# A first MLP product in two pieces: 256 tokens instead of 512 per matmul, in the last of six blocks

## The chip, the core and the metric

The kernel runs on one core of one Trainium2 chip. The metric is the device time of one execution in microseconds (us). Within the core five engines work side by side and meet through semaphores: TensorE (PE in the profile; its weight loads have a row of their own, PEld), VectorE (DVE), ScalarE (ACT), GpSimd (POOL) and SyncE (SP), which starts most of the transfers. Matmul results go to PSUM, which holds eight banks of 128 partitions by 512 fp32 values; everything else lies in SBUF or in DRAM.

## What is computed

The reference has two parts. The first is a Mamba-2 style state-space mixer over inputs of batch 4, 8 heads, 768 tokens, head size 32, state size 16. Cut to its core:

```python
for c in range(nc):                       # chunks of 32 tokens
    cum = np.cumsum(la, axis=-1)
    L = np.exp(cum[:, :, :, None] - cum[:, :, None, :]) * causal
    M = np.einsum('bhin,bhjn->bhij', Cc, Bc) * L
    y = np.einsum('bhij,bhjd->bhid', M, xc) + C_state_term
    state = decay_full * state + sum_of_outer_products
```

Its result, rearranged to 3072 tokens by 256 features, goes through an MLP with a hard-swish:

```python
h = x @ w_in                              # 3072 x 256 @ 256 x 2048
g = h * np.clip(h + 3.0, 0.0, 6.0) / 6.0
return g @ w_out                          # 3072 x 2048 @ 2048 x 256
```

Inputs are fp32 (the weights arrive as 64-bit floats and are decoded on the chip), and the output is fp32.

## The kernel before, in words

**Blocks.** The 768 tokens of each batch row are cut into `NC` = 6 blocks of 128, so a block holds `TB` = 512 tokens (4 batch rows by 128). Block k's mixer output `yTs[k]` is 256 features by 512 tokens, as two halves j = 0, 1 of 128 features. The 2048 hidden features are `NF` = 16 groups f of 128. While block k's MLP runs, the mixer of block k+1 is woven into it. The order on every engine is written out by hand in the loop at the end of the function (line 1030 on); nothing reorders it but the semaphores between engines.

**First MLP product.** Block 0 multiplies plain fp32 operands (`mlp_in`, line 626). Blocks 1 to 5 do it differently. `in_parts` splits each weight tile into three tiles of type F32R (`hi`, `lo`, `less`), and `split_y` does the same to the block's activations. A product of two F32R tiles is recorded as one matmul, a product of two plain fp32 tiles as two. Three such products are summed in one PSUM bank for each f: hi by hi and lo by lo (`squares`, line 696), and, after the bank has been scaled in place by `enlarge` (ACT at line 711, or DVE at line 708 for every fourth f), less by less (`cross`, line 713). Each of the three goes over j = 0, 1, so a group f takes 6 matmuls of 128x128 weights against 512 tokens, and a block 16 x 6 = 96. All of them are issued by `part_products`, line 692.

**After it.** `factor` turns the bank into the activated value: `ramp` on ACT (line 730) writes `gT`, `times_ramp` on DVE (line 735) multiplies it by the bank. Six banks are used in turn (f mod 6).

**Order in a block.** For f = 2 to 15 the loop at line 1084 issues `squares(k, f)`, `cross(k, f - 2)`, `enlarge(k, f)`, `factor(k, f - 2)`. The first two groups of a block are begun at the end of the block before it, by `lead` and `lead_on` (hi by hi, then lo by lo and the scaling): 8 matmuls for f = 0, 1.

**Second MLP product.** It is a Strassen-like scheme in which 7 products stand for 8, with sums of `gT` made on POOL (`g_sums`, line 796) and sums of `w_out` made once on DVE. Blocks 1 to 4 use `wide_units` (tiles wa, wb, wc, line 874, 256 columns per matmul). The last block uses `out_units` (tiles oa, ob, line 810, 128 columns per matmul): its activations are the stationary operand, so that its results need no turning and go straight out. It runs after the last `squares`, and the last two output transfers and one DVE addition (line 851) follow its last matmul.

**What the change touches.** `part_products` alone, called by `squares`, `cross`, `lead` and `lead_on`, for k = 5.

Of the kernel before, what the change touches and what calls it, by code (L numbers as in the profile page):

```python
# [21 lines left out]
def kernel(  # L22
# [24 lines left out]
    nc = tc.nc  # L47
    P = 128
# [3 lines left out]
    NC = S // P  # L52
    TB = NB * P
# [68 lines left out]
    FP = NF // NP  # L122
# [32 lines left out]
    def conceal_in(t, pattern):  # L155
# [24 lines left out]
        out=head, in_=head, pattern=[[-2 * N, NQ], [-N, 2]], compare_op=ALU.is_ge,  # L180
        fill=0.0, base=0, channel_multiplier=1)
    nc.gpsimd.affine_select(
        out=head, in_=head, pattern=[[2 * N, NQ], [N, 2]], compare_op=ALU.is_ge,
# [456 lines left out]
    w_parts, y_parts, hs_ = {}, {}, {}  # L640
# [47 lines left out]

    def part_products(k, f, n, m, start=False):
        w, y = w_parts[f // FP][n], y_parts[k][m]  # L690
        for j in range(NK):
            nc.tensor.matmul(  # L692
                out=hs_[k, f], lhsT=w[j][:, f % FP * P:(f % FP + 1) * P], rhs=y[:, j],
                start=(start and j == 0), stop=True, skip_group_check=True)

    def squares(k, f, low=True):

        pool, tag = ((ps, "f0"), (ps, "f1"), (ps, "f2"), (ps, "f3"), (ps_y, "y0"), (ps_y, "y1"))[f % 6]
        hs_[k, f] = pool.tile([P, TB], FP32, name="h", tag=tag)
        part_products(k, f, 0, 0, start=True)  # L700
        if low:
            part_products(k, f, 1, 1)
# [10 lines left out]
    def cross(k, f):  # L713
        part_products(k, f, 2, 2)
# [461 lines left out]
```

## Time and profile before

| what | value |
|---|---|
| three runs | 343.15, 343.79 (median), 344.34 us |
| profiled execution, its own time | 343.4 us |
| its span in the profile | 341.7 us |
| PE busy | 333.8 us, 98% of the span, 3372 matmul records and as many weight loads |
| DVE, ACT, POOL busy | 210.7, 188.3, 145.4 us |
| granted PE clock | 1.0 for the whole core |
| chain that ended last | PE 94% of the span; line 692 alone 33% |

A matmul record's duration covers the whole passage through the array, and records overlap: 480 records of line 692 last about 0.4 us each, but follow each other every 0.23 us. What a matmul costs in a dense row is therefore read from the chain that ended last (so many pieces of one line in so many us), not from the mean duration in the table of groups. The chain lists stretches as start, length, engine, tile, line and number of instructions. In the table of groups, `x160 | 51.8, 409 | 0.0` means 160 instructions, 51.8 us busy, 409 ns each, and no idle time before them. Weight loads are recorded the same way, in rows of PEld.

### The profile page before, as it was taken

How to read it: one execution, taken by the hardware profiler on the slowest of the kernel's cores; microseconds unless marked ns; L12 is line 12 of the kernel's file. 1: busy time of each engine (PE TensorE's matmuls, PEld its weight loads, DVE VectorE, ACT ScalarE, POOL GpSimd, SP SyncE). 2: the span in 40 equal slices, each digit the busy share in tenths (PEclk: the TensorE clock that was granted, in tenths of full speed). 3: DMA queues.
4: the chain of work that ended last, by engine and by line, in shares of the span. 5: the costliest groups of instructions: out<-in, count | busy, mean ns of one | idle time of the engine just before them, and what ended most of it. 6: DMA issues, size and time to landing. Idle time of an engine off the chain costs nothing.

```text
span 341.7 us, 8203 instructions
## 1 busy us (share of the span) xinstructions
PE 333.8 (98%) x3372; PEld 267.5 (78%) x3372; DVE 210.7 (62%) x332; ACT 188.3 (55%) x394; POOL 145.4 (43%) x139
## 2 busy tenths in 40 slices
PE   5999999999999999999999999999999999999996
PEld 2554448888878888888888888888888888888996
DVE  6699999996499739665519465528465323465011
ACT  4778878667987481675471676470576030576000
POOL 3300000381282998099803089810089600079600
PEclk9999999999999999999999999999999999999999
DMA  8989967052690216167107294001260001110000
GB/s 172 174 312 197 209 233 153 2 59 69 164 114 8 58 55 119 25 84 70 24 27 144 33 96 62 16 2 18 33 75 2 2 4 17 30 17 2 0 33 31
DMA packets 89605, 25.15 MB, mean 74 GB/s; under 512 B 82208, under 2 KB 85952, under 8 KB 89056
## 3 DMA queue, kind: packets, MB, share of 16 engines
q1 hardware_dynamic: 85184, 23.33, 36.5%
q10 hardware_dynamic: 4384, 1.31, 1.8%
q8 instruction: 26, 0.43, 0.5%
q14 instruction: 11, 0.09, 0.1%
HBM read 21.33 MB, written 3.29 MB: 72 GB/s over the span
## 4 chain that ended last, share of the span: by engine, by line
PE 94%; DMA 3%; DVE 1%; SPq 1%; issue 0%; DVEq 0%
PE h L692 33%; PE wb L874 13%; PE wc L874 8%; PE o L748 8%; PE h L626 8%; PE wa L874 8%; PE oa L810 4%; PE ob L810 4%; PE y L604 3%; PE y L503 2%; PE cb L530 2%; DMA raw<-in_moe_w_in_dram 2%; PE y L544 1%; DMA pairs<-in_C_dram 1%; SPq L101 1%; DVE L L574 0%
## 5 line engine op out<-in xcount | busy, mean ns | idle before, releaser
L735 DVE SCALAR_TENSOR_TENSOR gT<-gT,h 128x512 f32<-128x512 f32 x96 | 64.9, 686 | 41.1 <-ACT gT L730 39.9
L730 ACT ACTIVATE gT<-h,half 128x512 f32<-128x512 f32 x96 | 65.2, 684 | 17.8 <-PE h L692 15.9
L796 POOL TENSOR_TENSOR s<-gT 128x512 f32<-128x512 f32 x20 | 28.9, 1443 | 76.2 <-DVE gT L735 76.1
L711 ACT ACTIVATE h<-h 128x512 f32<-128x512 f32 x62 | 35.8, 583 | 43.6 <-PE h L692 39.3
L692 PE MATMUL h<-y_hi,w_part 128*128 128x512 f32 x160 | 51.8, 409 | 0.0
L692 PE MATMUL h<-y_less,w_part 128*128 128x512 f32 x160 | 49.7, 397 | 0.0
L692 PE MATMUL h<-y_lo,w_part 128*128 128x512 f32 x160 | 49.5, 395 | 0.0
L692 PEld LDWEIGHTS h<-y_lo,w_part 128*128 128x128 f32 x160 | 30.0, 188 | 7.4
L692 PEld LDWEIGHTS h<-y_less,w_part 128*128 128x128 f32 x160 | 30.0, 188 | 6.9
L692 PEld LDWEIGHTS h<-y_hi,w_part 128*128 128x128 f32 x160 | 30.0, 188 | 6.8 <-DVE gT L735 0.4
L385 ACT ACTIVATE L<-L,cum_n 128x64 f32<-128x64 f32 x128 | 31.6, 338 | 0.0
L874 PE MATMUL wb<-s,w_out 128*128 128x256 f32 x128 | 30.6, 382 | 0.0
L748 PE MATMUL o<-w_out,gT 128*128 128x256 f32 x128 | 28.8, 381 | 0.0
L626 PE MATMUL h<-yT,w_in 128*128 128x512 f32 x64 | 27.7, 594 | 0.0
L748 PEld LDWEIGHTS o<-w_out,gT 128*128 128x128 f32 x128 | 24.1, 190 | 3.8 <-issue 0.5
L403 POOL TENSOR_TENSOR tmp<-state,eto 128x256 f32<-128x256 f32 x5 | 3.4, 673 | 55.3 <-ACT eto L389 55.2
L874 PEld LDWEIGHTS wb<-s,w_out 128*128 128x128 f32 x128 | 24.0, 190 | 3.6
L796 POOL TENSOR_TENSOR s<-gT,s 128x512 f32<-128x512 f32 x20 | 26.0, 1306 | 1.3
L796 POOL TENSOR_TENSOR gT<-gT 128x512 f32<-128x512 f32 x20 | 25.7, 1291 | 1.3
L796 POOL TENSOR_TENSOR s<-s,gT 128x512 f32<-128x512 f32 x20 | 25.7, 1290 | 0.0
L158 POOL TENSOR_SCALAR_AFFINE_SELECT L<-L 64x1024 f32<-64x1024 f32 (+1 forms) x16 | 20.4, 1280 | 10.5 <-DMA L<-cum_d 10.1
L396 POOL TENSOR_TENSOR bs<-B,L 128x128 f32<-128x128 f32 x24 | 12.7, 545 | 26.0 <-ACT L L385 20.9
(138 smaller groups left out, 507.5 us busy)
## 6 DMA issues: line engine op xcount, KB each, us to landing
raw<-in_moe_w_out_dram SPq DMA_DIRECT2D x4, 1024.0 KB
L<-cum_d SPq DMA_DIRECT2D x8, 512.0 KB
xt<-in_x_dram SPq DMA_DIRECT2D x6, 512.0 KB
raw<-in_moe_w_in_dram SPq DMA_DIRECT2D x3, 1024.0 KB
out_dram<-back SPq DMA_DIRECT2D x128, 16.0 KB
pairs<-in_C_dram SPq DMA_DIRECT2D x40, 32.0 KB
eto<-cum_e SPq DMA_DIRECT2D x20, 64.0 KB
B<-in_B_dram SPq DMA_DIRECT2D x5, 256.0 KB
```

The source lines that it names most:

```text
L158: nc.gpsimd.affine_select(out=t[rows], in_=t[rows], pattern=pattern, compare_op=ALU.is_ge, fill=-1e5, base=base, channel_multiplier=-1)
L385: nc.scalar.activation(Ls[c][:, b, h], Ls[c][:, b, h], AF.Exp, bias=cum_n[:, c, g:g + 1])
L396: nc.gpsimd.tensor_tensor(out=bss[c][:, hs], in0=Bs[c][:, hs], in1=Ls[c][:, b, :, HT - 1:HT].to_broadcast([P, NH, N]), op=ALU.mult)
L626: nc.tensor.matmul(out=h, lhsT=w_in[f // FP][:, j, f % FP * P:(f % FP + 1) * P], rhs=yTs[k][:, j].rearrange("p b i -> p (b i)"), start=(j ...
L692: nc.tensor.matmul(out=hs_[k, f], lhsT=w[j][:, f % FP * P:(f % FP + 1) * P], rhs=y[:, j], start=(start and j == 0), stop=True, skip_group_ ...
L711: nc.scalar.activation(h, h, AF.Copy, scale=1.0 / EPS + 1.0)
L730: nc.scalar.activation(gTs[k][:, f], h, AF.Relu, bias=half, scale=1.0 / 6.0)
L735: nc.vector.scalar_tensor_tensor(out=g, in0=g, scalar=1.0, in1=h, op0=ALU.min, op1=ALU.mult)
L748: nc.tensor.matmul(out=o[:, b % 2], lhsT=gTs[0][:, f, b * P:(b + 1) * P], rhs=w_out[:, f], start=(f == 0 and b % 2 == 0), stop=True, skip_ ...
L796: nc.gpsimd.tensor_tensor(out=o, in0=p_, in1=q_, op=op)
L810: nc.tensor.matmul(out=bank[:, slot], lhsT=lhs[:, j], rhs=rhs[:, j], start=(clear and j == 0), stop=True, skip_group_check=True)
L874: nc.tensor.matmul(out=bank[:, slot], lhsT=lhs[:, j], rhs=rhs[:, j], start=(clear and j == 0), stop=True, skip_group_check=True)
```

## The change

For the last block, k = NC - 1 = 5, each of `part_products`' matmuls over 512 tokens becomes two over 256 tokens. Both use the same 128x128 weights, one directly after the other; the first writes columns 0 to 255 of the PSUM bank and the second columns 256 to 511. The bank is cleared for a new sum by the very first of the four pieces of hi by hi alone. In blocks 1 to 4 nothing changes. The number of matmuls of line 692 in block 5 goes from 96 to 192; the sums, their order per element, and all instructions of other engines are as before.

```diff
     def part_products(k, f, n, m, start=False):
         w, y = w_parts[f // FP][n], y_parts[k][m]
+        cuts = 2 if k == NC - 1 else 1
         for j in range(NK):
-            nc.tensor.matmul(
-                out=hs_[k, f], lhsT=w[j][:, f % FP * P:(f % FP + 1) * P], rhs=y[:, j],
-                start=(start and j == 0), stop=True, skip_group_check=True)
+            for t in range(cuts):
+                tokens = slice(t * TB // cuts, (t + 1) * TB // cuts)
+                nc.tensor.matmul(
+                    out=hs_[k, f][:, tokens], lhsT=w[j][:, f % FP * P:(f % FP + 1) * P],
+                    rhs=y[:, j, tokens], start=(start and j == 0 and t == 0), stop=True,
+                    skip_group_check=True)
```

## The prediction

> **What bounds the kernel now.** I read the page's first part, then the chain that ended last, then the groups of PE and PEld by shape.
>
> ```profile
> PE 333.8 (98%) x3372; PEld 267.5 (78%) x3372; DVE 210.7 (62%) x332; ACT 188.3 (55%) x394; POOL 145.4 (43%) x139
> ```
>
> PE is busy for 98% of the span, and there is one weight load per matmul record: 3372 of each. A busy PE need not be a bound PE, so the chain has to say whether anything else paces it. First two stretches from earlier blocks, then everything from the end of block 4 (columns: start, length, engine, tile, line, number):
>
> ```profile
> 22.61 27.66 PE h L626 x64
> ...
> 106.24 1.73 PE wa L874 x8
> ```
>
> ```profile
> 289.47 1.87 PE h L692 x8
> 291.33 1.73 PE wb L874 x8
> 293.06 19.96 PE h L692 x86
> 313.01 1.56 PE oa L810 x14
> 314.58 0.47 PE h L692 x2
> 315.04 3.79 PE oa L810 x34
> 318.84 1.79 PE ob L810 x16
> ...
> 336.70 1.80 PE oa L810 x16
> 338.50 0.02 issue
> 338.53 0.42 DVE res L851
> ```
>
> The last 49 us are PE without a gap, then one DVE addition, then the last transfer to the end at 341.7. Block 5's first MLP product is the 8 + 86 + 2 = 96 records of line 692, 1.87 + 19.96 + 0.47 = 22.30 us, so 232.3 ns from one to the next. Nobody holds PE up there: in 293 to 313 us ACT is busy 14.3 and DVE 12.3 of 20 us, and the longest entries of the list of waits in this stretch are these engines waiting for PE:
>
> ```profile
> ACT h L711 <- PE h L692: 10.3, 11, 6.2
> ...
> DVE gT L735 <- ACT gT L730: 8.7, 11, 1.2
> ```
>
> So what PE spends more on line 692 goes to the end of the run in full, and what it saves comes off in full, until another engine gets in the way.
>
> **What a record costs.** The loads and matmuls by shape (count, busy us, mean ns, idle us):
>
> ```profile
> L692 PEld LDWEIGHTS h<-y_hi,w_part 128*128 128x128 f32 x160 | 30.0, 188 | 6.8 <-DVE gT L735 0.4
> ...
> L604 PEld LDWEIGHTS y<-L,xt 64*32 64x32 f32 x768 | 8.6, 105 | 3.5 <-issue 2.4 <-ACT yT L618 0.7 <-DVE state L554 0.3
> ...
> L810 PEld LDWEIGHTS oa<-w_out,gT 128*128 128x128 f32 x64 | 7.5, 192 | 0.2
> ...
> L336 PEld LDWEIGHTS <-ident_h 128*128 128x128 bf16 x8 | 1.1, 136 | 3.7 <-issue 2.0 <-DVE ident_h L168 1.7
> ```
>
> Three readings.
> First, the pitch (distance from one start to the next) of two-record fp32 products: 1.79/16 = 112 ns at 128 columns, 1.73/8 = 216 at 256, 27.66/64 = 432 at 512. The slope is (432 - 216)/256 = 0.84 ns per column, and what is left over is 1 to 5 ns.
> Second, a one-record F32R product of 512 columns takes 232 ns. It cannot stream as slowly as 0.84 ns per column (430 ns); at half that, 0.42 (an estimate from the slope above), its stream is 215 ns at most, 213 with the 1 to 5 ns taken off, and 19 ns per product remain. These 19 ns are the disputed thing. No F32R product of another width is in the trace, so whether they belong to the product or to its columns is not seen.
> Third, the loads. A 128-column fp32 load lasts 188 to 192 ns, one of 32 columns 105: (188 - 105)/96 = 0.86 ns per column, 111 ns for 128 columns, and some 77 ns that overlap with others, since line 810 takes a new load every 112 ns.
>
> **The change, part by part.**
> *Stream.* 192 records of 256 columns in place of 96 of 512: the same columns, so 0 us.
> *Added fixed part.* 96 more records. If the 19 ns belong to each record (its start, or the load that runs beside it), a piece takes 213/2 + 19 = 125.5 ns, a pair 251, and the change 96 x 19 = +1.8 us. If they belong to the columns, only the 1 to 5 ns of the fp32 rows come with each added record: at 2.5 ns, 96 x 2.5 = +0.24 us. Low end: a piece as fast as line 810's record with its own load, 112 ns: 96 x (224 - 232) = -0.8 us; with the fastest full-width record that has a load (the transposes of line 422, 0.87 us for 8, 109 ns): 96 x (218 - 232) = -1.3 us. High end: a piece that waits for a whole load record, 188 ns: 96 x (376 - 232) = +13.8 us.
> I take +1.8, because the nearest rows speak for a cost per record: records of line 692 differ by tile and not by what the other engines do (by the start times in the timeline some 235 ns for y_hi, 232 for y_lo, 229 for y_less, in every block alike), which looks like the operands of a load and a stream meeting each other, once per load. With 213 ns of stream the 111 ns of load cover half of it; with 107 they cover all of it, but it is the same 111 ns of overlap per record.
> *Added loads.* 96 more of 128 columns. That a repeated load is not left out is seen at line 336: eight products with one and the same `ident_h` have eight loads. Each needs 111 to 112 ns, and a piece of 125 ns covers it, barely. I price it at nothing beyond the 19; the cover is 13 ns per piece.
> *Order and waits.* No wait is added: a bank is released to ACT by the last piece of a group, as by the last product before. On PE's queue 192 more instructions (96 matmuls, 96 loads) pass; at lines 604 and 530 records follow each other at 15 to 18 ns (0.79/53 and 0.98/55 in the chain), so issue isn't near a limit. No DMA is added, and SP's and POOL's queues see nothing new. ACT, DVE and POOL are all paced by PE here, so they run as much later as PE does. Line 810's rows follow directly, with POOL's sums in the same distance behind the last `factor` as before.
> *Where it lands.* 8 of the 96 products lie at 289.5 us, inside block 4's second product; there PE bounds too. The tail after the last matmul (0.42 us DVE, then the transfer) is unchanged.
>
> Sum: +1.8 us on the profiled execution, span 341.7 to 343.5, its time 343.4 to 345.2. The profiled execution lies 0.4 us under the median of the three runs, 343.79; for the median the forecast is 345.6.
>
> **A rule against the row.** The Trainium skill, page "TensorE: Matmul & The Clock Gate", section "Back-to-back issue gap", gives an isolated warm matmul N/2.4 + 2.5 ns. For 512 columns that is 216 ns, and this trace shows 232 for F32R, so the trace does not agree for these products. By the rule the change would cost 2.5 ns per added record, 0.24 us, against 1.8 us by the row, and the time would be 344.0, as in the first rival below.
>
> **The rivals.**
> *The 19 ns belong to the columns* (not slower than can be measured). If F32R streams at 0.45 ns per column, halving the width costs only the 2.5 ns: 344.0 us, +0.07%. For it: nothing in the trace separates the two. Against it: the pitch differs by 6 ns between tiles of equal shape, and a per-column rate should not.
> *Faster.* If the 19 ns are something that a 512-column record meets once late in its stream, pieces run at 109 to 112 ns and PE is 0.8 to 1.3 us earlier: 342.5 to 343.0 us. It gains once a piece is under 116 ns, and passes 0.3% once it is under 110.8. For it: rows at 109 and 112 with full loads. Against it: those rows stream at half the data rate.
> *The load becomes the bound.* The load of a piece can start only when the piece before has begun, and if a load beside a full-rate stream needs more than 125 ns, pieces wait for it. Halfway between 125 and 188, some 150 ns, this is 96 x (300 - 232) = +6.5 us, 350.3; at the whole record +13.8, 357.6. For it: load and stream are now equally long. Against it: the load's record in line 692 lasts 188 ns beside a full-rate stream and 192 beside the slower one of line 810, so the stream does not stretch it. The far end of this rival is that load and stream add up: 111 + 107 + 2.5 = 220 ns per piece, 96 x (440 - 232) = +20 us, 363.8; I give that 0.02 of its 0.12, since line 810 has full-height loads every 112 ns beside 107 ns of stream.
> The same page of the Trainium skill, section "What overlaps and what doesn't", says that a load overlaps with running matmuls only where row groups differ, which is this far end; line 810's 112 ns disagree with it.
> *The second load isn't made.* Then the change isn't quite what it says: a pair has one 19 and one 2.5, 344.0 us again. Against it: line 336.
>
> **How the numbers follow.** Cost per record 0.60 (345.1 to 346.1, as the excess is 13 to 23 ns by tile); per column 0.14; no second load 0.04; load-bound 0.12; faster 0.10. A measurement of this kernel can tell about 0.3%, 1.03 us, from no change. Slower by more: 0.60 + 0.12 = 0.72. Faster by more: the half of the faster case that passes 1.03 us, and a little for the spread of runs, 0.07. Within: 0.14 + 0.04 + 0.03 = 0.21. The range reaches from the per-column case less the spread of the runs (344.0 - 0.4 = 343.6) to 347.8, a piece of 137 ns, halfway from 125 to the load-bound case's 150; that leaves out 0.10 below and some 0.08 above. The likeliest case's own range is 345.1 to 346.1.
>
> **What would show it.** In the profile after, line 692 has 256-column records, 192 of them, and as many loads more than before as matmuls (3468 of each). The chain's stretch that starts near 293 us is 21.6 us long with some 172 pieces, 125 ns each. At 116 ns the per-column case is right, at 112 or less the faster one, above 130 the load bounds. The out_units stretch of 25.5 us and the tail are as before; a gap in it, or ACT or POOL releasing PE there, would make the forecast wrong in another way, as would a granted clock below 1.0.

## The result, and the profile after

In ten runs each the kernel took 344.87 us (median) against 343.81 before: a ratio of 1.0035, with a 95% interval of 1.0019 to 1.0051. Timed a second time it was 344.38 against 343.81, ratio 1.0016 (1.0005 to 1.0028). One of the twelve executions of that second timing ran at a granted clock of 0.756 and took 423.85 us; the median and the ratio leave it out, and every ratio here compares all the other executions, not the medians alone. The changed kernel is slower, by some two to three parts in a thousand. The profiled execution took 344.21 us, its span 342.5.

The page's first part of the changed kernel: 96 more matmul records, 96 more loads, and nothing new on the other engines.

```profile
PE 333.9 (97%) x3468; PEld 272.3 (80%) x3468; DVE 211.7 (62%) x332; ACT 188.5 (55%) x394; POOL 145.5 (42%) x139
```

The chain that ended last, from the end of block 4 (start, length, engine, tile, line, number; `part_products` is line 695 now, the last product line 814):

```profile
289.67 1.91 PE h L695 x16
291.59 1.73 PE wb L878 x8
293.31 20.49 PE h L695 x172
313.81 1.56 PE oa L814 x14
315.37 0.48 PE h L695 x4
315.85 3.79 PE oa L814 x34
...
339.31 0.02 issue
339.33 0.42 DVE res L855
```

Block 5's first product is 192 records in 1.91 + 20.49 + 0.48 = 22.88 us, 119.2 ns each; before it was 96 in 22.30 us, 232.3 each. So the pieces cost +0.58 us, or 6.1 ns for each of the 96 added records. All later stretches are as long as before, and PE is still without a gap. The span grew by 0.8 us. The other 0.2 us were there before block 5 began: its first record starts at 289.67 instead of 289.47. The experiments come back to it.

The pieces by shape:

```profile
L695 PE MATMUL h<-y_hi,w_part 128*128 128x256 f32 x64 | 10.4, 287 | 0.0
L695 PE MATMUL h<-y_less,w_part 128*128 128x256 f32 x64 | 10.2, 284 | 0.0
L695 PE MATMUL h<-y_lo,w_part 128*128 128x256 f32 x64 | 10.0, 282 | 0.0
...
```

```profile
L695 PEld LDWEIGHTS h<-y_hi,w_part 128*128 128x128 f32 x64 | 8.8, 189 | 0.1
L695 PEld LDWEIGHTS h<-y_less,w_part 128*128 128x128 f32 x64 | 8.8, 192 | 0.0
```

Three times 64 matmuls of 256 columns, each with its own load of 128 columns. PEld's idle time in front of these loads is gone: a load has only the time of its own piece now.

### The profile page after: what moved, and what is told of

Same layout as the page of the kernel before. It is cut to its first block, busy times and chain, and to the rows that moved or that the text cites. A ratio compares the mean times of both kernels' runs of the same rounds, so it can differ in the third digit from the quotient of the medians.

```text
span 342.5 us, 8406 instructions
## 1 busy us (share of the span) xinstructions
PE 333.9 (97%) x3468; PEld 272.3 (80%) x3468; DVE 211.7 (62%) x332; ACT 188.5 (55%) x394; POOL 145.5 (42%) x139
## 4 chain that ended last, share of the span: by engine, by line
PE 94%; DMA 3%; DVE 1%; SPq 0%; issue 0%; DVEq 0%
PE h L695 33%; PE wb L878 13%; PE wc L878 8%; PE o L752 8%; PE h L626 8%; PE wa L878 8%; PE oa L814 4%; PE ob L814 4%; PE y L604 3%; PE y L503 2%; PE cb L530 2%; DMA raw<-in_moe_w_in_dram 2%; DMA pairs<-in_C_dram 1%; PE y L544 1%; SPq L101 0%; DVE L L574 0%
## 5 line engine op out<-in xcount | busy, mean ns | idle before, releaser
L695 PE MATMUL h<-y_hi,w_part 128*128 128x512 f32 (+1 forms) x192 | 51.8, 368 | 0.0
L695 PE MATMUL h<-y_less,w_part 128*128 128x512 f32 (+1 forms) x192 | 50.2, 360 | 0.0
L695 PE MATMUL h<-y_lo,w_part 128*128 128x512 f32 (+1 forms) x192 | 49.7, 358 | 0.0
L695 PEld LDWEIGHTS h<-y_lo,w_part 128*128 128x128 f32 x192 | 32.7, 188 | 5.9
L695 PEld LDWEIGHTS h<-y_less,w_part 128*128 128x128 f32 x192 | 32.8, 189 | 5.5
L695 PEld LDWEIGHTS h<-y_hi,w_part 128*128 128x128 f32 x192 | 32.8, 188 | 5.4
L626 PEld LDWEIGHTS h<-yT,w_in 128*128 128x128 f32 x64 | 12.1, 190 | 14.9 <-issue 13.2
```

Of the source, the lines that this page charges most:

```text
L626: nc.tensor.matmul(out=h, lhsT=w_in[f // FP][:, j, f % FP * P:(f % FP + 1) * P], rhs=yTs[k][:, j].rearrange("p b i -> p (b i)"), start=(j ...
L695: nc.tensor.matmul(out=hs_[k, f][:, tokens], lhsT=w[j][:, f % FP * P:(f % FP + 1) * P], rhs=y[:, j, tokens], start=(start and j == 0 and t ...
```

## The experiments

Two theories stood against each other first. *By columns:* a record costs 6 ns plus 0.442 ns per column, from the two widths measured, and its load is hidden. *By the load:* 119 ns are what one load takes beside a full-rate stream, and the pieces already wait for it. Below, "block 5" means the records of `part_products` in block 5, summed from the chain as above; before the change it took 22.30 us, with it 22.88.

**Pieces of 128.**

```diff
-        cuts = 2 if k == NC - 1 else 1
+        cuts = 4 if k == NC - 1 else 1
```

> Four pieces of 128 tokens per product in block 5: 384 records in place of 96. Two theories stand after the change's profile, in which 192 pieces of 256 took 22.88 us, 119.2 ns each. By columns: a record costs 6 ns plus 0.442 ns per column (232.3 = r + 512 c, 119.2 = r + 256 c), loads hidden as long as they fit; a piece streams 63 ns, but a 128-column load takes 111 to 112 ns (line 810), so the pieces go at 112: 384 x 112 = 43.0 us, +20.7 us on before. By the load: the 119 ns are already the time of one F32R load beside a full-rate stream, so the pieces go at 119 again: 45.8 us, +23.5 us. If repeated loads of the same weights cost nothing, 384 x 63 = 24.2 us, +1.8 us.

The median was 364.63 us against 344.23, ratio 1.0600 (1.0584 to 1.0615). The chain of this run:

```profile
289.78 3.52 PE h L695 x32
...
295.08 38.36 PE h L695 x344
...
335.05 0.84 PE h L695 x8
```

Block 5 took 42.72 us, 111.3 ns a piece. That is what the loads of line 810 had shown before (112), not 119 and not the 63 of the stream alone. A 128-column F32R load needs 111 ns of its own even beside full-rate streams, and it is made again for the same weights. So pieces of 256, at 119 ns, have time for their loads, though only 8 ns are left over; the run with half loads, further down, bears this out.

**Pieces of 384 and 128.**

```diff
-        cuts = 2 if k == NC - 1 else 1
+        cuts = ((0, 384), (384, TB)) if k == NC - 1 else ((0, TB),)
...
-            for t in range(cuts):
-                tokens = slice(t * TB // cuts, (t + 1) * TB // cuts)
+            for t0, t1 in cuts:
+                tokens = slice(t0, t1)
...
```

> Block 5's products cut at token 384: pieces of 384 and 128. Both theories let the 384 piece stream 6 + 170 = 176 ns. By columns, the 128 piece waits for a load of 112 ns: a pair 288, +5.3 us on before. By the load, its load takes 119: a pair 295, +6.0 us. If a load fits beside the 384 piece and the one for the next product does not need the whole 128 piece, as little as 238 a pair, +0.6 us.

349.48 us against 344.23, ratio 1.0158 (1.0139 to 1.0176).

```profile
289.56 2.24 PE h L695 x16
...
293.58 24.65 PE h L695 x172
...
319.85 0.53 PE h L695 x4
```

Block 5 took 27.42 us, 285.6 ns a pair: 111 for the short piece (its time is its successor's load) and 175 for the long one, where 6 + 0.442 x 384 gives 176. The start times of the loads in the trace show the same division: they lie 108 and 178 ns apart by turns (medians). The line through 256 and 512 columns holds at 384, and the floor of a load is seen again. In block 5's records, this uneven cut costs about nine times what the even one does (5.12 against 0.58 us).

**The same pieces, weights alternating.**

```diff
-        for j in range(NK):
-            for t in range(cuts):
+        for t in range(cuts):
+            for j in range(NK):
```

> The same 192 pieces of 256 in block 5, but over j inside the halves, so that no weights come twice in a row. If a repeated load costs what any load costs, 119 ns a piece as in the change: 22.9 us for line 692's products of block 5, +0.6 us in the profile. If loading the same weights again is cheaper, pieces are slower here, up to 125 ns: +1.7 us. If it is dearer, they come down towards 116: no difference to before.

344.69 us against 344.23, ratio 1.0016 (1.0004 to 1.0027), block 5 22.87 us (1.90, 20.49 and 0.48). The same weights twice in a row are neither cheaper nor dearer than others.

**The cut in all five blocks, and the change again.** The change's median had risen by more than its pieces explain.

```diff
-        cuts = 2 if k == NC - 1 else 1
+        cuts = 2
```

> The cut in two in blocks 1 to 5: 480 added records. In the change's profile the 96 added records cost 0.58 us of block 5, while the median of the runs rose by 1.06. If 6 ns per added record is all there is, +2.9 us. If the other 0.5 us belong to the records too, and the profiled execution was a lucky one, 5 x 1.06 = +5.3 us. If they come once per program, from its start, +3.4 us. By the forecast of 19 ns per record it would be +9 us.

> The change as it is, timed again, since its first median stood 1.06 us above before while its profile shows 0.58 us in line 695's products of block 5, and the same 192 pieces with alternating weights stood only 0.46 us above. If the 0.58 us are all, the ratio is 1.0017; if something besides the pieces costs, it stays at 1.003.

All five blocks: 346.94 us against 344.23, +2.7, ratio 1.0084 (1.0071 to 1.0097), which is 480 x 5.6 ns; in its trace each of the five blocks' products takes 22.87 to 22.93 us. The change again: ratio 1.0016, as block 5's 0.58 us (0.17%) alone would give. So neither run shows a second cost; that the first timing stood higher is put down here to the spread between executions, which is argued and not shown.

Part of that spread is seen at the first stretch of block 0's product, which is 27.66 us long in every run and begins at another time. Before, in the changed kernel, and in the changed kernel's second profile:

```profile
20.13 0.17 issue
...
22.61 27.66 PE h L626 x64
```

```profile
20.12 0.73 issue
...
23.17 27.66 PE h L626 x64
```

```profile
23.78 27.66 PE h L626 x64
```

In the first two the chain is level until 20.1 us. There PE stands for 0.73 in place of 0.17 us without a wait that the profile shows, and block 0's product begins 0.56 us later. Of this, 0.20 is left when block 5 begins; most of the rest, 0.25, is made up in block 1's first product, whose records take 22.56 us in the profile before and 22.33 in the other. In the second profile PE was already 1.0 us late ahead of that piece. What delays PE there is not shown. Such a shift of up to 1.2 us between executions is twice what the change costs.

**What the 6 ns and the 0.442 ns are made of.** The five runs from here on were executed once each, so only the lengths in their traces are compared. In the runs so far, the products of blocks 2 to 4, where they are not cut, take 22.27 to 22.33 us; differences under some 0.06 us mean nothing. First, loads of half the columns, at 512 tokens (with `cuts = 1`) and at 256:

```diff
+        n_w = P // 2 if k == NC - 1 and n else P
...
-                    out=hs_[k, f][:, tokens], lhsT=w[j][:, f % FP * P:(f % FP + 1) * P],
+                    out=hs_[k, f][:n_w, tokens], lhsT=w[j][:, f % FP * P:f % FP * P + n_w],
```

> Pieces of 512 in block 5 as before, but the lo by lo and less by less products load only 64 of their 128 weight columns, so the lower half of the partitions alone gets these two small corrections (that part of the computation is left out for the upper half). Four of six records then stream beside a load of 64 columns. If what a record takes over 0.417 ns per column comes from the load running beside it, these four come down from 232 to some 223 ns: block 5's products 22.3 - 0.6 = 21.7 us. If it is the stream's own rate, all stay at 232 and 22.3 us.

> The change's 192 pieces of 256 in block 5, with 64 of 128 weight columns loaded in the lo by lo and less by less products (the upper half of the partitions goes without these two small corrections). If the load beside a piece sets its 119 ns, some 126 of the 192 pieces fall towards 110: block 5's products 22.9 - 1.1 = 21.8 us. If 6 ns per record and 0.442 ns per column are the stream's own, 22.9 us.

At 512 tokens nothing changed:

```profile
290.43 1.85 PE h L696 x8
...
294.01 19.94 PE h L696 x86
...
315.51 0.47 PE h L696 x2
```

This is 22.26 us, 231.9 ns a record. At 256 it did:

```profile
290.00 1.88 PE h L696 x16
...
293.61 20.01 PE h L696 x172
...
315.18 0.47 PE h L696 x4
```

22.36 us, 116.5 ns a piece. With weights of 64 columns in two thirds of the records, cutting costs 22.36 - 22.26 = 0.10 us, some 1 ns per added record instead of 6. So most of the 6 ns needs full weights. Neither theory had this.

It is tempting to say that a full load beside a short piece slows it. The start times in this trace do not bear that out. From one start to the next (medians), the pieces of `y_hi`, whose weights stay whole, take 119 to 121 ns, those of `y_lo` 116 to 117, those of `y_less` 113 to 115; in the change's trace all three take 117 to 120. While the last piece of `y_less` in a group runs, the whole weights of the next `y_hi` are loaded, and it still takes 114 ns on average. While the last piece of `y_hi` runs, half weights are loaded, and it still takes 118. (Both take some 120.5 in the change's trace.) So the saving goes mainly with the piece's own weights, and the 119 ns are not the time of the next piece's load. What it is about full weights stays open: a piece with 64 of its 128 columns also writes 64 partitions of its PSUM bank instead of 128.

Then bf16 operands in place of F32R, the activations first read as two bytes of every four, whole and in pieces of 256, and then from a packed copy:

```diff
+                w_j, y_j = (t.bitcast(BF16).rearrange("p (n two) -> p n two", two=2)[:, :, 1]
+                            for t in (w_j, y_j))
...
```

> Block 5's products at 512 tokens with the upper halves of the F32R words taken as bf16 for both operands, so that the words' lower halves are left out of these products. Tokens lie at the same addresses, two bytes of every four are read, and the load is of another kind. If the 0.442 ns per column belong to four-byte operands, records come down from 232 to about 216 ns (the shortest distance of line 348's bf16 records): 20.8 us in block 5, -1.5 us. If they belong to the stream of any type at full rate, 232 stays.

> As the run with bf16 operands (the lower halves of the F32R words left out of block 5's products), which took 21.56 us at 512 tokens, 225 ns a record, but in pieces of 256. Its loads last 97 ns instead of 188. If the 5 to 7 ns that a 256 piece of F32R takes over half of 225 come from the four-byte load beside it, bf16 pieces take 112.5 ns and block 5's products stay at 21.6 us. If they come with any record, 192 x (112.5 + 6) = 22.7 us.

> As the run with bf16 operands at 512 tokens, but all of block 5's products move one packed bf16 copy of the activations (written by ACT in place of the less part, so the lo and less parts of the activations are left out). If the 0.439 ns per column came from reading two bytes of every four, packed tokens stream at 216 ns a record: 20.8 us in block 5. If any one-record stream in a dense row goes at 0.439, 21.6 us.

The first of the three, in the chain:

```profile
289.71 0.68 PE h L695 x3
290.39 0.07 issue
290.46 1.06 PE h L695 x4
...
293.25 8.37 PE h L695 x37
301.62 0.07 issue
301.68 11.02 PE h L695 x48
...
314.26 0.23 PE h L695
314.49 0.07 issue
314.55 3.96 PE oa L813 x34
```

Three records are missing from this trace (3 + 4, 37 + 48 and 1 are 93 of 96), and the "issue" pieces and 0.17 us of the last stretch (3.96 instead of 3.79 us) stand in for them. So block 5 is 1.81 + 19.46 + 0.47 = 21.74 us, 226 ns a record; the 21.56 us and 225 ns in the next run's expectation had left these 0.17 us out. In pieces of 256:

```profile
290.30 1.82 PE h L698 x16
...
293.84 19.55 PE h L698 x172
...
314.95 0.46 PE h L698 x4
```

This is 21.83 us, 113.7 ns each, again 1 ns per added record, although all 128 partitions of the bank are written; so that alone does not cost the 6 ns. The records of the loads last 97 ns there instead of 188. The packed copy:

```profile
290.29 0.65 PE h L699 x3
290.94 0.05 issue
290.99 1.03 PE h L699 x4
...
293.74 7.99 PE h L699 x37
301.73 0.05 issue
301.78 10.52 PE h L699 x48
```

86 records in 18.56 us (7.99 + 0.05 + 10.52), 216 ns each: tokens packed in two bytes stream 10 ns faster per 512 than the same number of tokens spaced four bytes apart. That is 0.02 ns per column. The packed run also reads one copy for all three products where the spaced one reads three tiles; but those three do not differ from each other (226 ns each by the start times).

Put together, and as an estimate from these runs: an F32R record of 512 columns in this kernel is 216 ns as for packed bf16, 10 for the spacing of its tokens, and 6 that remain, 232. One of 256 is 108, half of 216 (packed pieces were not run), 5 for the spacing, and 6 that remain, 119. That four-byte tokens pay for their spacing as spaced bf16 tokens do is taken over from the bf16 runs, not shown for F32R. At 256 columns the last 6 fall to between 3 and 4 on average where two thirds of the weights are halved, and to less than 1 with bf16 operands. At 512, halved weights don't lower them; why is not settled.

## Why the prediction was right or wrong

*What bounds the kernel:* right, though of the two waits shown for it only the first is a wait for PE. The second is DVE waiting for ACT, and the longest of that list is POOL waiting for DVE (30.2 us). None is PE waiting, so the reading stands. PE paced everything from block 4's end on, no other engine got in the way, and the 0.58 us of block 5 reached the end in full; the cut in all blocks moved the time by 2.7 us where its records give 5 x 0.58 = 2.9.

*Stream, loads, order, tail:* right as to the sum. Repeated loads are made, each in 111 ns, and a piece covers one; that the columns cost the same in either width fits the three widths measured. The cover that I put at 13 ns is 8, and with pieces of 128 it is gone and costs 20.4 us. The "load becomes the bound" rival was thus one halving away. Its far end, load and stream adding up to 220 ns, did not occur, which also contradicts the rule of the Trainium skill's page "TensorE: Matmul & The Clock Gate" (section "What overlaps and what doesn't") that was weighed there: 119 ns a piece and 111 ns with pieces of 128 were measured with full-height loads running beside the matmuls.

*Added fixed part:* the sign was right and the size wrong by three. I took the 19 ns that an F32R record needs over 213 as the price of each added record: +1.8 us. Measured: 6.1 ns, +0.58 us. By the bf16 runs some 10 of the 19 ns go with the columns, because the tokens lie four bytes apart, as the first rival had it for all of them; only some 6 come with each record, and most of these with full four-byte weights. So the step that was mis-sized is the choice to give all 19 ns to the record. The argument for it, that pitches differing by tile speak against a rate per column, was not enough: both parts were in the number. What the same page's section "Back-to-back issue gap" gives for 512 columns, 216 ns, agrees with the packed bf16 records (216) and with neither kind of tokens four bytes apart (226 and 232); the 2.5 ns for an added record that follow from it are neither the 6 of F32R nor the 1 of the spaced bf16 pieces.

*The numbers:* the medians of 344.87 and 344.38 us lie in the range of 343.6 to 347.8 and under the likeliest case's own 345.1 to 346.1. That the range holds them is owed to its low end, which came from the first rival, and the first timing's +1.06 us came nearer to +1.8 than the pieces' 0.58 us by the luck of the spread. That the kernel is slower holds against no change, at 0.35% and 0.16%, about and below the 0.3% that I named as the limit of one measurement; one profile's start alone moves by up to 1.2 us.

## What to carry to other kernels

What a record takes beyond its ideal stream is not one number: measure it at two widths before it is multiplied by the number of added records. In this kernel a 128-column load of four-byte weights needs 111 ns of its own. Pieces of 256 columns stream longer than that, and cutting into them is nearly free (6 ns for each added record); with pieces of 128 the load sets the time. Weights that repeat are loaded again and save nothing. Cut evenly: beside a short piece a whole load still has to be made, and the long piece does not give that time back.

## What the runs showed of the hardware that was not expected

- Tokens four bytes apart stream slower than packed two-byte tokens: 226 against 216 ns per 512 bf16 columns, with loads of the same length (97 and 98 ns) and at a granted clock of 1.0.
- Full four-byte weights cost a piece of 256 columns some 5 ns, though the load's own time, 111 ns, is shorter than the piece's 119: an added record costs 6 ns with them, and 1 ns with bf16 operands or with two thirds of the weights halved. By the start times it goes mainly with the piece's own weights and not with the load that runs beside it: 114 ns for a half-weight piece beside a whole load, 118 for a whole-weight piece beside a half load.
- Loading the same weights again straight away costs what loading others does: 22.87 and 22.88 us for the same 192 pieces.
